# A causal attention and a squared-ReLU MLP on one core: another table of rank shifts for the scheduler

## The chip, the core and the metric

The kernel runs on one core of a Trainium2 chip. The metric is the device time of one execution in microseconds. Three runs of the kernel before gave 607.66, 607.70 and 609.86 us, a median of 607.7. The profiled execution is one more.

## The reference

`q`, `k` and `v` are float32 of shape (4, 12, 448, 64): four batches, twelve heads, 448 positions, 64 numbers a head. The MLP takes 1792 tokens of 768 numbers, with `w_in` (768 x 2048) and `w_out` (2048 x 768), which are float64 in the kernel's memory.

```python
scores = scale * np.matmul(q, k.transpose(0, 1, 3, 2))
mask = np.triu(np.ones((seq, seq), dtype=bool), k=1)
scores = np.where(mask, -1000000000.0, scores)
attn = np.exp(scores - np.max(scores, axis=-1, keepdims=True))
attn = attn / (np.sum(attn, axis=-1, keepdims=True) + 1e-09)
x = np.matmul(attn, v)          # heads side by side: (1792, 768)
h = np.maximum(x @ w_in, 0.0)
out = h * h @ w_out
```

## The kernel before

**Work.** Two heads (of 64) are handled together and called a head here, numbered 0 to 23; heads 0 to 11 belong to batches 0 and 1, 12 to 23 to batches 2 and 3. For a head, Q and K are loaded and turned over (on VectorE, `transposed`, or for some heads on TensorE, `turned_rows`); TensorE makes the scores in seven chunks of 64 queries (`softmax`, two steps of chunks for heads 0 to 11, one for the others); for each chunk VectorE adds the mask and takes the row maximum and ScalarE takes the exponential and its row sum (`exponential`); VectorE takes the reciprocals of the sums (`inverse`), GpSimd multiplies by them (`normalise`), TensorE turns P over (`transposed_p`), ScalarE or VectorE copies it out of PSUM, and TensorE multiplies by V (`times_v`).

The MLP runs on numbers that are split into a high and a low part (`split`), so that each product is three matmuls: high x high, high x low, low x high. The weights come in pieces (`piece`: a load, two conversions on ScalarE, three steps on VectorE, the split). For batches 0 and 1 the MLP is done directly, in four groups of 512 hidden columns (`h_unit`, lines 679 to 681, and `o_unit`, lines 1098 to 1100). For batches 2 and 3 a scheme of seven products in place of eight is used (`h_pair`, lines 860 to 864; `o_parts`, `o_seven` and `o_last`, lines 986 to 988), whose weight sums are made by GpSimd's accumulating loads (`added_up`) and split again; for the output weights the low half of the split is GpSimd's alone. In time: heads 0 to 11 with the first products between them until about 105 us, then heads 12 to 23 between the rest of the direct MLP until about 370 us, then the scheme of seven.

**What sets the order.** No instruction is written in its place. Each step is told to a planner with `plan.op`: its rank, the engines that could do it (`ways`) with a cost, what it reads and writes, and which buffers it takes and frees. `Plan.emit` then picks one step after the other: among all steps whose inputs are planned to be there, the one that could start first, and among those that could start at the same time the one with the lowest rank. It chooses the engine that would end it first. Two-operand instructions of VectorE and of GpSimd are marked as sharing a port and planned one after the other. The picked steps, in order of planned start, become the instruction streams of the engines and the DMA queues; each engine then works its stream in order and waits by semaphore for what a step reads. The planner's costs only set the order; nothing holds an instruction back on the chip but its inputs and its place in the stream.

**The table.** A step's rank is worked out from its place in the kernel. Afterwards `AMENDS` adds to it: an entry (first, end, more) adds `more` to the steps first to end - 1, numbered in the order in which `plan.op` was called.

```python
    def amend(self, table):
        for first, end, more in table:
            for o in self.ops[first:end]:
                o.rank += more
...
                key = (w[1], o.rank)
                if best is None or key < best[0]:
                    best = (key, o, w)
```

Which steps the numbers are, counted from the code: 0 to 49 head 0 (13 and 14 its turned K and Q, 15 and 22 its two score steps, 31 its reciprocals, 32 to 38 its normalisations, 39 to 46 its turned P, 47 times V); 50 to 94 head 1 (60 and 67 its score steps, 61 to 66 and 68 to 75 its exponentials, 76 its reciprocals); 95 to 139 head 2; 140 to 189 head 3; up to 547 heads 4 to 11; from 549 the first weight piece; up to 1,698 the direct MLP; from there heads 12 to 23, from 2,287 the parts of x, and the scheme of seven in the order in which it runs, up to 3,429.

Of the kernel before, what the change touches and what calls it, by code (L numbers as in the profile page):

```python
# [190 lines left out]
def kernel(  # L191
# [1017 lines left out]
    for gr, u in stages:  # L1209
# [5 lines left out]
            W = w_parts(gr, u, rank - LEAD, rank + 7 * CB * H_US - LEAD)  # L1215
            rank = h_pair(gr, u, W, rank, H_US, last)
    AMENDS = (
# [15 lines left out]
    )  # L1233
    plan.amend(AMENDS)
    with tc.manual_schedule():
# [32 lines left out]
```

## Time and profile before

| what | value |
|---|---|
| median of three runs | 607.7 us |
| the profiled execution's own time | 607.55 us |
| its span, first to last instruction | 605.4 us |
| busy: TensorE matmul, VectorE, ScalarE, GpSimd | 97%, 71%, 60%, 59% |
| granted TensorE clock, mean | 0.996 |
| data moved by DMA | 120.01 MB |

The span is what the trace covers; the execution's own time has some 2 us more around it. Engines are PE (TensorE's matmuls), PEld (its weight loads, beside PE), DVE (VectorE), ACT (ScalarE), POOL (GpSimd) and SP (SyncE, which issues most DMAs). L679 is line 679 of the kernel. A busy time of TensorE is modelled at its ends, since matmuls overlap in the array: the distance of two starts is the pace, the duration is longer.

### The profile page before, as it was taken

What the parts mean: (1) busy time and instruction counts of PE and PEld (TensorE: products, weight loads), DVE (VectorE), ACT (ScalarE), POOL (GpSimd) and SP (SyncE); (2) the same over time, 40 slices, a digit from 0 to 9 for tenths busy, and PEclk for the clock granted to TensorE, in tenths of its full rate; (3) what the DMA queues carried; (4) which work ended last, traced back from release to release, by engine and by line L of the source; (5) the groups of instructions that cost most, each with busy time, mean ns of one, the idle gap of its engine ahead of it and who ended that gap; (6) DMA issues with size and microseconds to landing.
All of it is one profiled execution on the core that took longest, in us unless ns stands there. A gap on an engine that the chain in (4) does not pass through costs nothing.

```text
span 605.4 us, 11455 instructions
## 1 busy us (share of the span) xinstructions
PE 586.6 (97%) x3766; PEld 514.5 (85%) x3766; DVE 427.2 (71%) x948; ACT 360.9 (60%) x887; POOL 356.4 (59%) x465
## 2 busy tenths in 40 slices
PE   3899999999999999999999999999999999999996
PEld 2577877898988998888898889999799999999995
DVE  4888796466876687666676518698896798778453
ACT  3899997674688555667547742268656645642400
POOL 2475772865577755967567844157675667776000
PEclk9999999999999999999999999999999999999999
DMA  9899444979799979977998668979757946762564
GB/s 157 185 230 190 101 113 102 256 237 308 189 282 297 266 193 227 285 208 229 251 264 266 233 204 241 273 241 211 188 120 169 229 104 138 177 162 55 168 100 84
DMA packets 190651, 120.01 MB, mean 198 GB/s; under 512 B 126016, under 2 KB 178560, under 8 KB 190592
## 3 DMA queue, kind: packets, MB, share of 16 engines
q1 hardware_dynamic: 169488, 107.99, 64.3%
q0 software_dynamic: 6912, 9.44, 10.2%
q10 hardware_dynamic: 14192, 1.85, 1.9%
q8 instruction: 30, 0.49, 0.3%
q14 instruction: 29, 0.24, 0.1%
HBM read 80.71 MB, written 38.54 MB: 197 GB/s over the span
## 4 chain that ended last, share of the span: by engine, by line
PE 91%; DVE 4%; DMA 1%; ACT 1%; SPq 0%; issue 0%; ACTq 0%; DVEq 0%
PE ps L482 7%; PE ps L679 7%; PE ps L1098 7%; PE ps L462 7%; PE ps L680 6%; PE ps L681 6%; PE ps L1100 6%; PE ps L1099 6%; PE ps L422 6%; PE ps L986 6%; PE ps L988 5%; PE ps L987 5%; PE ps L864 5%; PE ps L862 5%; PE ps L860 5%; DVE r L321 1%
## 5 line engine op out<-in xcount | busy, mean ns | idle before, releaser
L318 ACT ACTIVATE words<-words 128x384 f32<-128x384 f32 (+3 forms) x134 | 76.7, 599 | 25.4 <-DVE words L321 13.1
L448 POOL TENSOR_SCALAR ap<-ap,asm 128x64 f32<-128x64 f32 (+6 forms) x122 | 76.7, 647 | 24.6 <-DVE asm L516 17.9
L435 DVE CUSTOM_DVE_ANT_0 ps<-ps,mask 128x320 f32<-128x320 f32 (+6 forms) x168 | 68.4, 446 | 24.9 <-PE ps L422 20.6
L1098 PE MATMUL ps<-wo,g 128*128 128x384 f32 x224 | 77.0, 344 | 0.0
L1100 PE MATMUL ps<-wo,g 128*128 128x384 f32 x224 | 75.2, 336 | 0.0
L1099 PE MATMUL ps<-wo,g 128*128 128x384 f32 x224 | 75.2, 336 | 0.0
L679 PE MATMUL ps<-x,wi 128*128 128x448 f32 x192 | 74.2, 386 | 0.0
L680 PE MATMUL ps<-x,wi 128*128 128x448 f32 x192 | 70.3, 366 | 0.0
L681 PE MATMUL ps<-x,wi 128*128 128x448 f32 x192 | 70.3, 366 | 0.0
L439 ACT ACTIVATE ap<-ps,mx 128x64 f32<-128x64 f32 (+6 forms) x126 | 58.5, 479 | 14.2 <-DVE mx L435 13.4
L325 POOL TENSOR_TENSOR wi<-words,wi 128x384 fp32r<-128x384 f32 (+1 forms) x51 | 62.8, 1260 | 6.7 <-ACT wi L318 4.3
L318 ACT ACTIVATE r<-ps 128x448 f32<-128x448 f32 x63 | 33.9, 543 | 45.7 <-PE ps L864 16.1
L986 PE MATMUL ps<-g,wi 128*128 128x448 f32 x156 | 57.3, 368 | 1.5 <-ACT sa L318 1.5
L987 PE MATMUL ps<-g,wi 128*128 128x448 f32 x156 | 57.0, 366 | 0.0
L988 PE MATMUL ps<-g,wi 128*128 128x448 f32 x156 | 57.0, 366 | 0.0
L864 PE MATMUL ps<-x,wi 128*128 128x448 f32 x153 | 56.1, 367 | 0.0
L862 PE MATMUL ps<-x,wi 128*128 128x448 f32 x153 | 56.1, 367 | 0.0
L860 PE MATMUL ps<-x,wi 128*128 128x448 f32 x153 | 56.1, 366 | 0.0
L640 DVE TENSOR_SCALAR words<-words 128x384 int32<-128x384 int32 (+1 forms) x56 | 29.0, 520 | 32.4 <-ACT words L318 30.5
L331 POOL TENSOR_SCALAR wi<-words 128x512 fp32r<-128x512 f32 (+1 forms) x31 | 20.3, 663 | 50.5 <-DVE words L643 31.6
L318 ACT ACTIVATE apt<-ps 128x512 f32<-128x512 f32 x68 | 38.1, 603 | 17.4 <-PE ps L462 17.0
L321 DVE CUSTOM_DVE_ANT_0 words<-words 128x768 uint16<-128x768 uint16 (+1 forms) x56 | 39.7, 709 | 6.9 <-ACT words L318 3.9
(146 smaller groups left out, 1481.4 us busy)
## 6 DMA issues: line engine op xcount, KB each, us to landing
words<-in_moe_w_in_dram SPq DMA_DIRECT2D x24, 512.0 KB, 5.3
words<-in_moe_w_out_dram SPq DMA_DIRECT2D x32, 384.0 KB, 4.1
wo_split<-wo SPq DMA_DIRECT2D x26, 384.0 KB, 5.0
wi<-wo_split SPq DMA_DIRECT2D x25, 384.0 KB, 4.0
wo_whole<-words SPq DMA_DIRECT2D x32, 192.0 KB, 4.0
wi_split<-wi SPq DMA_DIRECT2D x24, 256.0 KB, 3.8
v<-in_v_dram SPq DMA_DIRECT2D x24, 192.0 KB, 4.4
wi_whole<-words SPq DMA_DIRECT2D x18, 256.0 KB, 4.6
```

The costliest lines, as they stand in the source:

```text
L318: return (ACT, t_act(n, psum, more), lambda: nc.scalar.activation(dst(), src(), func, **kw))
L679: nc.tensor.matmul(o, w[:, 0], x[:, 0], start=c == 0, stop=False)
L680: nc.tensor.matmul(o, w[:, 0], x[:, 1], start=False, stop=False)
L681: nc.tensor.matmul(o, w[:, 1], x[:, 0], start=False, stop=c == NP - 1)
L860: nc.tensor.matmul(o, w.t[:, 0, c], x[:, 0], start=begin and c == 0, stop=False, skip_group_check=True)
L862: nc.tensor.matmul(o, w.t[:, 0, c], x[:, 1], start=False, stop=False, skip_group_check=True)
L986: nc.tensor.matmul(o, w.t[:, 0, d], g.t[:, 0], start=start, stop=False, skip_group_check=True)
L987: nc.tensor.matmul(o, w.t[:, 0, d], g.t[:, 1], start=False, stop=False, skip_group_check=True)
L988: nc.tensor.matmul(o, w.t[:, 1, d], g.t[:, 0], start=False, stop=stop, skip_group_check=True)
L1098: nc.tensor.matmul(res(), g[:, 0], w[:, 0], start=f == 0, stop=False)
L1099: nc.tensor.matmul(res(), g[:, 0], w[:, 1], start=False, stop=False)
L1100: nc.tensor.matmul(res(), g[:, 1], w[:, 0], start=False, stop=f == GF - 1)
```

## The change

The table is replaced; nothing else is. The old one has 77 entries, the new one 237 shorter ones, and many entries of the old one come back cut into parts with different values. Below are the lines that the prediction speaks of.

```diff
-        (0, 25, 5.5), (25, 62, 9.6), (62, 65, 1.1), (65, 71, -2.8), (71, 107, -3.8), (107, 111, -4.9),
-        (111, 132, -7.2), (229, 237, -5.7), (274, 282, 6.9), (355, 369, 14.8), (369, 375, 15.9),
...
-        (460, 472, 13.1), (472, 495, 7.3), (495, 509, 3.7), (509, 563, 1), (563, 592, 6), (592, 603, -4.4),
-        (603, 614, 8.4), (621, 637, 15.6), (637, 666, 5.4), (877, 901, 3.8), (901, 920, 14.3),
-        (920, 937, 7.2), (937, 943, 9.3), (966, 970, 4.8), (970, 1080, 0.6), (1080, 1088, 1.1),
...
-        (2187, 2237, -0.4), (2237, 2263, -14.2), (2450, 2466, -5.6), (2466, 3233, -6.9), (3233, 3410, 3.5),
+        (0, 25, 5.5), (25, 31, 9.6), (31, 44, 13.9), (44, 61, 9.6), (61, 62, -25.2), (62, 65, -33.7),
+        (65, 71, -37.6), (71, 72, -38.6), (72, 107, -8), (107, 111, -9.1), (111, 113, -11.4),
+        (113, 119, -0.3), (119, 121, 3.9), (121, 125, -7.2), (125, 132, -14.4), (132, 134, -7.2),
+        (134, 147, 6.1), (147, 148, 5.7), (148, 150, 22.8), (155, 156, 6.9), (156, 164, 1.8),
...
+        (485, 495, 14), (495, 509, 10.4), (509, 557, 7.7), (557, 563, 1), (563, 570, 6), (570, 576, -11.2),
...
+        (637, 645, 14.9), (645, 666, 35.4), (666, 676, 30), (676, 716, 2.1), (720, 722, 5.5),
...
+        (877, 886, -1.8), (886, 892, -13.6), (892, 901, -5), (901, 904, 5.5), (904, 911, -0.4),
+        (911, 918, -11.1), (918, 919, -1.9), (919, 920, -9.1), (920, 921, -9.6), (921, 934, -13.1),
...
+        (2450, 2455, -8.1), (2455, 2458, -6.3), (2458, 2466, 4), (2466, 2469, 2.7), (2469, 2534, -6.6),
+        (2534, 2555, -2.1), (2555, 2571, -24.3), (2571, 2578, -6.9), (2578, 2581, -11), (2581, 2585, -0.7),
+        (2585, 2590, -3.2), (2590, 2610, -19.1), (2610, 2613, -12.1), (2613, 2632, -19.1),
...
+        (2959, 3233, -12.1), (3233, 3410, -1.7), (3410, 3412, -5.2),
```

## Rows read from the trace of the kernel before

**Rows 1.** The page's first part: busy us, share of the span, instructions.

```profile
PE 586.6 (97%) x3766; PEld 514.5 (85%) x3766; DVE 427.2 (71%) x948; ACT 360.9 (60%) x887; POOL 356.4 (59%) x465
```

**Rows 2.** Windows: length, busy us and instructions of each engine, clock, DMA share, GB/s.

```profile
30.00:45.00 15.00, 15.00 (x162) 11.53 (x160) 13.10 (x45) 14.54 (x44) 11.85 (x22) 1.00 1.01 231
...
405.00:420.00 15.00, 15.00 (x76) 13.80 (x75) 12.68 (x21) 11.29 (x23) 11.22 (x15) 1.00 0.95 233
420.00:435.00 15.00, 13.56 (x66) 11.91 (x64) 15.00 (x17) 9.79 (x19) 12.15 (x14) 1.00 0.86 201
...
465.00:480.00 15.00, 15.00 (x76) 13.84 (x75) 13.25 (x17) 9.83 (x20) 10.89 (x14) 1.00 0.92 201
...
600.00:606.00 6.00, 0.00 (x0) 0.00 (x0) 1.20 (x4) 0.22 (x1) 0.00 (x0) 0.79 0.37 77
```

**Rows 3.** Waits of TensorE: waiter <- what ended it: us, times, longest.

```profile
PE ps L422 <- DVE aqt L403: 6.8, 1, 6.8
PE ps L422 <- DVE asm L515: 3.4, 1, 3.4
PE ps L986 <- ACT sa L318: 1.5, 1, 1.5
```

**Rows 4.** Timeline of TensorE, first 45 us: start, us, instruction, count, idle before.

```profile
13.23 3.26 PE L422 MATMUL ps<-bkt,bqt 64*64 64x320 f32 x28 [3.38 <-DVE asm L515]
...
28.61 1.95 PE L482 MATMUL ps<-bpt,v 128*64 128x448 f32 x16
...
33.90 1.47 PE L462 MATMUL ps<-ident,ap 128*128 128x128 f32 x12
35.30 1.75 PE L422 MATMUL ps<-akt,aqt 64*64 64x448 f32 x28
36.98 1.95 PE L482 MATMUL ps<-apt,v 128*64 128x448 f32 x16
38.86 0.60 PE L389 MATMUL ps<-ident,rows 112*128 112x112 f32 x4
```

**Rows 5.** Timeline of VectorE at the start.

```profile
17.64 0.64 DVE L403 STREAM_TRANSPOSE aqt<-aq 128x448 f32<-128x448 f32 x1
18.21 0.60 DVE L435 CUSTOM_DVE_ANT_0 ps<-ps,mask 128x448 f32<-128x448 f32 x1
```

**Rows 6.** Timeline of ScalarE at the start.

```profile
19.19 0.60 ACT L318 ACTIVATE apt<-ps 128x512 f32<-128x512 f32 x1
19.66 0.65 ACT L439 ACTIVATE bp<-ps,mx 128x448 f32<-128x448 f32 x1
```

**Rows 7.** Matmuls by line: count, busy us, mean ns of one, idle before.

```profile
L679 PE MATMUL ps<-x,wi 128*128 128x448 f32 x192 | 74.2, 386 | 0.0
L681 PE MATMUL ps<-x,wi 128*128 128x448 f32 x192 | 70.3, 366 | 0.0
L1098 PE MATMUL ps<-wo,g 128*128 128x384 f32 x224 | 77.0, 344 | 0.0
L1100 PE MATMUL ps<-wo,g 128*128 128x384 f32 x224 | 75.2, 336 | 0.0
```

**Rows 8.** Timeline of VectorE, 408 to 440 us.

```profile
425.67 0.61 DVE L321 TENSOR_TENSOR g<-f,g 128x448 fp32r<-128x448 f32 x1
426.21 4.12 DVE L321 TENSOR_TENSOR r<-r,f 128x448 f32<-128x448 f32 x1
...
432.39 3.06 DVE L321 TENSOR_TENSOR r<-r,r 128x448 f32<-128x448 f32 x1
```

**Rows 9.** Timeline of GpSimd there: the first and the last of three.

```profile
426.57 1.34 POOL L325 TENSOR_TENSOR wi<-words,wi 128x384 fp32r<-128x384 f32 x1
...
428.50 1.33 POOL L325 TENSOR_TENSOR wi<-words,wi 128x384 fp32r<-128x384 f32 x1
```

**Rows 10.** Timeline of ScalarE there.

```profile
434.46 0.52 ACT L318 ACTIVATE sa<-ps 128x448 f32<-128x448 f32 x1
```

45 rows, old and new, of the table AMENDS are left out of this document.

## The prediction

> **What bounds the kernel now.** I read the page's first two parts, then a table of 15 us windows, then the waits of TensorE, then the timelines of the two places where TensorE waits. TensorE works 586.6 of the 605.4 us of the span [rows 1]. The window table says where the rest is: all 26 windows from 30 to 420 us show it busy 15.00 of 15.00, the first and the last of them stand in the group, and so do the nine from 450 to 585; 420 to 435 lacks 1.44, and the last 5.4 us of the span have no matmul at all [rows 2]. Its waits are few: 6.8 us until the first transposed Q is there, 3.4 us before head 1's scores, 1.5 us late in the kernel behind a copy of ScalarE [rows 3]. So the profiled execution is 2.15 us outside the span (607.55 less 605.4), 6.8 before the first matmul, about 593.2 of TensorE from there to 600.0, and 5.4 of tail. The number of matmuls does not depend on the table: only what keeps them apart can move. (607.55 stands 0.15 below the median of 607.7; the sum below is against 607.55.)
>
> Three things keep them apart. **The start.** From head 1's scores at 13.23 to head 1's product with V at 28.61 are 15.38 us. TensorE does 68 score matmuls there (two heads and 12 of a third), 32 transposes, one product with V and 8 transposes of rows. Later the same work starts at a settled pace: 28 scores in 36.98 - 35.30 = 1.68, a product with V in 38.86 - 36.98 = 1.88, 12 transposes in 35.30 - 33.90 = 1.40, and 4 row transposes last 0.60 [rows 4]. That makes 68 x 0.060 + 32 x 0.117 + 1.88 + 1.2 = 10.9, so 4.5 us are waiting inside the start, beside the 3.4 ahead of it. **Breaks.** The first matmul of a triple that can follow a break lasts longer: L679 386 ns against L681's 366, x192, is 3.8 us; L1098 344 against L1100's 336, x224, is 1.8 us [rows 7]. Together 5.6 us hang on how often the order switches TensorE between attention and products. **The late wait.** At 426.21 VectorE's subtraction takes 4.12 us and at 432.39 its addition 3.06, where its neighbour of the same shape takes 0.61 [rows 8]; beside the first of them three two-operand instructions of GpSimd lie end to end, 426.57 to 429.83 [rows 9]. ScalarE's queue stands behind VectorE's results, so its copy of a finished PSUM bank to `sa` starts only at 434.46 [rows 10], and TensorE waits 1.46 of its 1.5 us of [rows 3] for that bank.
>
> **The change part by part.** I number the steps in the order in which the program calls `plan.op` and subtract the old table from the new one, step by step. 1,919 of 3,430 steps get another rank, by 7.8 on average up or down. No operation is added or removed; the rank decides only between steps that the planner could start at the same time, so a shift changes an order, or nothing, or (where two engines may take the step) the engine.
>
> (a) Start, steps 0 to 189 (heads 0 to 3). Head 1's exponentials and its second score step (61 to 71) go forward by 34.8, to ranks between -25 and -13, ahead of everything there. Head 0's reciprocal, its seven normalisations and most of its P transposes (31 to 43) go back by 4.3. Head 2's exponentials 113 to 120 go back by 6.9 to 11.1, head 2's Q and K transposes forward by 4.2, and the first weight piece (549 to 556) back by 6.7. Today VectorE does head 2's Q transpose (17.64) before the last and widest row maximum of head 1 (18.21) [rows 5], and ScalarE copies a transposed P of head 0 (19.19) before head 1's last exponential (19.66) [rows 6]. With the new ranks both swap: the exponential goes from 19.66 to 19.19, 0.47 earlier, and with it head 1's reciprocal, the GpSimd normalisations behind it and the transposes that wait for them. One more row maximum of head 2 (0.30 us) now stands behind head 3's Q transpose instead of ahead of it. 0.47 + 0.30 gives -0.8, which I take. The ends: at best all 4.5 us of waiting go; at worst a step that went back (head 0's normalisations, head 2's exponentials, the weight piece) makes TensorE wait once more, and the nearest row to such a wait is the 3.4 us ahead of head 1's scores [rows 3]. So -4.5 to +3.4. I stay near the rows that swap. The cover for the weight piece is attention itself: TensorE comes to the first triple of products only after head 1's product with V.
>
> (b) The steps of 30 to 405 us: group 0's second half later by 30 (645 to 675), group 1's first products earlier by 9 to 25 (886 to 933), the second batches' heads 12 to 23 shifted one by one. TensorE is never idle there [rows 2] because products fill what attention leaves; the cover is the stock of ready products, and the window just before the end of the first twelve heads is as full as the rest. A step moved there earns nothing unless it changes the number of breaks. I take 0, between -1.4 (a quarter of the 5.6 us of breaks gone, my estimate) and +1.4 (a quarter more). DMA issues on SyncE's queue move too (heads 3, 6, 7, 15, 18 to 20); what waits behind them is the same filler-covered attention, so 0 as well, with the same ends.
>
> (c) The late wait. The GpSimd instructions at 426.57 to 429.83 are the low halves of weight sums of the first output turn; with the rest of that chain, its accumulating loads included (2590 to 2631), they go forward by 12.2 (three of them by 5.2), from ranks 435 to 438 to 423 to 426. VectorE's subtraction that they hold up has rank 430 before and after. So where the planner put GpSimd behind VectorE's chain it now puts it ahead, and the activations of the next pair (2555 to 2570), which stand before the `sa` copies on ScalarE's queue, go forward by 17.4 while the additions they wait for (2534 to 2554) go back by 4.8. The planner sees a GpSimd instruction and a two-operand VectorE one as sharing a port, and with the new ranks it plans the wait instead of meeting it. I take the 1.46 us of TensorE's wait as gone: -1.5. Ends: -1.5, and +3.5 if another such run of three lands in the chain (4.12 less 0.6 [rows 8]). VectorE is busy without a gap from 420 to 435 (15.00 of 15.00 [rows 2]), so there is no cover for a further one.
>
> The Trainium skill, "SBUF — State Buffer", section "SBUF: two separate sides", says that VectorE with two SBUF inputs and GpSimd share one port pair by an exclusive lock held for a whole instruction, and that the loser waits until it ends. Read as one instruction at a time, that would make the 4.12 us about 1.6 (0.6 and one of the three at their spacing of 0.97), and a further collision would cost about 1.0 instead of 3.5; the trace agrees that one blocks the other but not on the length, since one VectorE instruction waited out three [rows 8, 9].
>
> (d) After step 2,959 (from 475 us): one shift of -5.2 for all up to 3,411. A common shift swaps nothing, TensorE is full there, and the last 18 steps, which make the tail of 5.4 us, are not in either table: 0.
>
> Sum: -0.8 + 0 - 1.5 + 0 = -2.3; 607.55 - 2.3 = 605.2.
>
> **Rivals.** A, more of the waiting goes: half of the start's 4.5 (2.2), the late 1.5 and a quarter of the breaks (1.4) make -5.1: 602.4. For it: the entries lie thick exactly where these rows are. Against: the 3.4 us ahead of head 1's scores cannot move, since head 0's exponentials and head 1's transposes on VectorE keep their ranks.
> B, the order moves and the time does not: ScalarE waits for something else at 434, and the start is paced by the work of VectorE and ScalarE whatever its order: 607.5. For it: 26 full windows. Against: the two swaps of (a) need no luck.
> C, slower: the run of GpSimd instructions, moved ahead, falls into VectorE's gapless chain at 412 to 432 once more. Today's two blocked instructions cost VectorE 3.5 + 2.5 = 6.0 us and TensorE 1.46, so the cushion between them is some 4.5 us; it is used up, and each further run of three costs 3.5: 611.0 with one, 614.5 with two. It decides from the point where VectorE loses more than 6.0 us to blocked instructions before 435. For it: the shift sends these instructions into a stretch where every VectorE instruction is of the two-operand kind. Against: the planner serialises the two.
>
> **How the numbers follow.** Forecast 605.2, chance 0.38, its own range 603.9 to 606.6. A 0.27, B 0.18, C 0.17. A measurement here can tell about 0.5% from no change: 604.7 and 610.7 against 607.7. A is faster, B the same, C slower; of the forecast's own range about a third lies under 604.7. Faster 0.27 + 0.12 = 0.39, same 0.26 + 0.18 = 0.44, slower 0.17. From 601.5 to 610.5 leaves out C and a small part of A, 2 in 10.
>
> **What would show it.** (a): head 1's last exponential ahead of the P copy on ScalarE, and the product with V of head 1 before 28.0. (b): the means of L679 and L1098 within 5 ns of now, all windows from 30 to 405 at 15.00. (c): no wait of TensorE behind ScalarE's `sa` copy; if VectorE instructions of over 1.5 us before 435 sum to more than today, C. (d): last stretch and tail as before, 5.4 us without a matmul. The prediction is wrong if TensorE idles in a window that is full now, or if the breaks change by more than a quarter.

## The result, and the profile after

| | before | changed |
|---|---|---|
| median in the comparison | 609.10 us (607.66 to 611.50) | 603.58 us (603.15 to 606.17) |
| ratio, 95% interval | | 0.9914 [0.9885, 0.9943] |
| the profiled execution's own time | 607.55 us | 606.17 us |
| its span | 605.4 us | 604.3 us |

The changed kernel is 0.57 to 1.15% faster. The profiled execution shows less of it than the medians do: of before it is shorter than all six timed runs, of the changed kernel it is the longest of six. So the changed kernel was run and profiled once more (604.73 us, span 603.0), and below both traces of it are read.

Busy time of the changed kernel, as in [rows 1]: TensorE's is the same, VectorE and GpSimd have each 8 us less.

```profile
PE 587.0 (97%) x3766; PEld 513.8 (85%) x3766; DVE 418.8 (69%) x951; ACT 361.8 (60%) x889; POOL 348.1 (58%) x460
```

Its windows, as in [rows 2]. From 420 to 435 TensorE is now full and VectorE no longer is (13.09 of 15.00), but four windows that were full no longer are: 30 to 45 lacks 0.59, 45 to 60 lacks 0.44, and 405 to 420 and 465 to 480 some 0.3 each. (In the second trace 30 to 45 lacks 0.27 and 405 to 420 lacks 0.38.)

```profile
30.00:45.00 15.00, 14.41 (x138) 10.86 (x139) 13.59 (x44) 13.48 (x43) 10.98 (x20) 1.00 0.97 205
45.00:60.00 15.00, 14.56 (x146) 10.84 (x144) 11.86 (x39) 14.70 (x46) 7.62 (x13) 1.00 1.01 181
...
405.00:420.00 15.00, 14.70 (x72) 13.16 (x72) 12.24 (x21) 11.44 (x24) 9.20 (x11) 1.00 0.90 223
420.00:435.00 15.00, 15.00 (x75) 13.60 (x74) 13.09 (x20) 11.46 (x24) 9.63 (x13) 1.00 0.89 210
...
465.00:480.00 15.00, 14.74 (x73) 13.32 (x72) 8.64 (x15) 7.46 (x16) 7.80 (x10) 1.00 0.71 176
```

TensorE's waits, as in [rows 3]. The wait behind ScalarE's copy to `sa` is gone. New are a wait of 0.6 at L679 for a copy of ScalarE (at 32 us), two waits for a load of split weights, and one for `sb` just before the end.

```profile
PE ps L1063 <- DVE sb L321: 0.5, 1, 0.5
...
PE ps L860 <- DMA wi<-wi_split: 0.3, 1, 0.3
...
PE ps L986 <- DMA wi<-wo_split: 0.3, 1, 0.3
```

At the start ScalarE does what was forecast: head 1's last exponential (18.94) stands ahead of the copy of head 0's P (19.84); in [rows 6] it was the other way round. (The last one is another chunk now: step 75, 128 wide, in place of step 62, 448 wide.) TensorE's product with V of head 1 starts at 27.03, not 28.61 [rows 4].

```profile
18.94 0.37 ACT L439 ACTIVATE bp<-ps,mx 128x128 f32<-128x128 f32 x1
...
19.84 1.10 ACT L318 ACTIVATE apt<-ps 128x512 f32<-128x512 f32 x2
```

```profile
27.03 1.95 PE L482 MATMUL ps<-bpt,v 128*64 128x448 f32 x16
```

The breaks, as in [rows 7], are what they were: 386 and 343 ns.

```profile
L1098 PE MATMUL ps<-wo,g 128*128 128x384 f32 x224 | 76.8, 343 | 0.0
...
L679 PE MATMUL ps<-x,wi 128*128 128x448 f32 x192 | 74.1, 386 | 0.6 <-ACT aqt L318 0.6
```

VectorE's late sums, 400 to 605 us (count, busy us, mean ns of one). First before, then the changed kernel: 12 of them took 1,349 ns on average, now 11 take 679, where one that nothing holds up takes some 610. The longest from 408 to 440 us was 4.12 [rows 8] and is 2.33.

```profile
L321 DVE TENSOR_TENSOR r<-r,r 128x448 f32<-128x448 f32 x12 | 16.2, 1349 | 0.1
```

```profile
L321 DVE TENSOR_TENSOR r<-r,r 128x448 f32<-128x448 f32 x11 | 7.5, 679 | 0.1
```

```profile
422.02 2.33 DVE L321 TENSOR_TENSOR f<-f,r 128x448 f32<-128x448 f32 x1
```

The tail, on VectorE, before and then the changed kernel (its second trace). Before, a sum and a turn of another output block (599.56 and 600.22) stand between the last product's sum and the two copies that end the chain. In the changed kernel they are not there any more.

```profile
598.34 0.69 DVE L321 TENSOR_TENSOR sb<-ps,sb 128x256 f32<-128x256 f32 x2 [1.74 <-PE ps L988]
599.56 0.62 DVE L321 TENSOR_TENSOR sb<-ps,sb 128x448 f32<-128x448 f32 x1 [0.53 <-PE ps L988]
600.22 0.65 DVE L1036 STREAM_TRANSPOSE words<-sb 128x448 f32<-128x448 f32 x1
600.79 0.44 DVE L1072 COPY words<-ps 128x128 f32<-128x128 f32 x2
```

```profile
597.95 0.69 DVE L321 TENSOR_TENSOR sb<-ps,sb 128x256 f32<-128x256 f32 x2 [1.13 <-PE ps L988]
599.16 0.48 DVE L1072 COPY words<-ps 128x128 f32<-128x128 f32 x2 [0.53 <-PE ps L1063]
```

**Where the time goes, of ten kernels alike.** For each step on TensorE I took its start in the timeline, less the sum of the settled durations of all steps ahead of it (0.61 us for a triple of first-product matmuls, 1.88 for a product with V, and so on; 574.35 in all). What is left, the lag, grows only where TensorE loses time. The table has the first matmul, what the lag grew by in four stretches (the first one without the first matmul), and the time behind the last matmul; a row adds up to the span less 574.8 (574.35 and some 0.4 for the last step itself).

| kernel | first matmul | to 60 us | 60 to 405 | 405 to 495 | 495 to the end | tail |
|---|---|---|---|---|---|---|
| before | 6.75 | 11.37 | 4.90 | 2.26 | -0.05 | 5.46 |
| before, again | 6.92 | 11.15 | 4.91 | 2.24 | -0.04 | 5.46 |
| changed | 6.73 | 11.39 | 5.07 | 1.66 | 0.88 | 3.81 |
| changed, again | 7.20 | 10.35 | 5.08 | 0.86 | 0.86 | 3.83 |
| tail_swap | 7.18 | 11.35 | 4.91 | 3.18 | 0.68 | 3.83 |
| spread | 7.37 | 10.83 | 5.36 | 1.71 | -0.05 | 5.46 |
| graft_late | 6.99 | 11.37 | 4.88 | 1.25 | 0.87 | 3.82 |
| two_edits | 7.27 | 11.39 | 4.91 | 1.63 | 0.69 | 3.83 |
| early_turn | 7.03 | 10.95 | 5.09 | 1.09 | 0.87 | 3.82 |
| start_only | 7.14 | 12.42 | 6.94 | 1.71 | 6.66 | 5.65 |

The kernels of the table that are not named so far are those of the experiments. Two more, middle_only and late_only, read in the same way, lose 6.9 and 8.3 us from 405 to 495.

### The profile page after: what moved, and what is told of

The parts are those of the page before. It is cut to its first block, busy times and chain, and to the rows that moved or that the text cites. A ratio compares the mean times of both kernels' runs of the same rounds, so it can differ in the third digit from the quotient of the medians.

```text
span 604.3 us, 11456 instructions
## 1 busy us (share of the span) xinstructions
PE 587.0 (97%) x3766; PEld 513.8 (85%) x3766; DVE 418.8 (69%) x951; ACT 361.8 (60%) x889; POOL 348.1 (58%) x460
## 4 chain that ended last, share of the span: by engine, by line
PE 90%; DMA 4%; ACT 2%; SPq 2%; issue 1%; DVE 0%; ACTq 0%; DVEq 0%
PE ps L1098 7%; PE ps L679 7%; PE ps L1100 6%; PE ps L1099 6%; PE ps L681 6%; PE ps L680 6%; PE ps L482 6%; PE ps L462 6%; PE ps L986 6%; PE ps L988 6%; PE ps L987 6%; PE ps L422 5%; PE ps L860 5%; PE ps L864 5%; PE ps L862 5%; DMA words<-in_moe_w_in_dram 2%
## 5 line engine op out<-in xcount | busy, mean ns | idle before, releaser
L318 ACT ACTIVATE words<-words 128x384 f32<-128x384 f32 (+3 forms) x140 | 79.8, 597 | 27.9 <-DVE words L321 15.3
L448 POOL TENSOR_SCALAR ap<-ap,asm 128x64 f32<-128x64 f32 (+6 forms) x123 | 74.6, 626 | 30.6 <-DVE asm L516 27.7
L435 DVE CUSTOM_DVE_ANT_0 ps<-ps,mask 128x448 f32<-128x448 f32 (+6 forms) x168 | 68.4, 446 | 19.2 <-PE ps L422 12.9
L679 PE MATMUL ps<-x,wi 128*128 128x448 f32 x192 | 74.1, 386 | 0.6 <-ACT aqt L318 0.6
L439 ACT ACTIVATE ap<-ps,mx 128x448 f32<-128x448 f32 (+6 forms) x126 | 59.2, 487 | 15.0 <-DVE mx L435 11.1
L325 POOL TENSOR_TENSOR wi<-words,wi 128x384 fp32r<-128x384 f32 (+1 forms) x44 | 52.6, 1204 | 11.8 <-ACT wi L318 6.6
L986 PE MATMUL ps<-g,wi 128*128 128x448 f32 x153 | 56.0, 366 | 0.3 <-DMA wi<-wo_split 0.3
L987 PE MATMUL ps<-g,wi 128*128 128x448 f32 x153 | 56.0, 366 | 0.0
L988 PE MATMUL ps<-g,wi 128*128 128x448 f32 x153 | 56.0, 366 | 0.0
L331 POOL TENSOR_SCALAR wi<-words 128x384 fp32r<-128x384 f32 (+1 forms) x39 | 26.9, 689 | 46.6 <-DVE words L643 23.0
L321 DVE CUSTOM_DVE_ANT_0 words<-words 128x768 uint16<-128x768 uint16 (+1 forms) x56 | 42.3, 755 | 5.8 <-ACT words L318 3.3
L318 ACT ACTIVATE apt<-ps 128x512 f32<-128x512 f32 x65 | 35.6, 611 | 14.5 <-PE ps L462 14.4
```

The source lines that it names most:

```text
L318: return (ACT, t_act(n, psum, more), lambda: nc.scalar.activation(dst(), src(), func, **kw))
L679: nc.tensor.matmul(o, w[:, 0], x[:, 0], start=c == 0, stop=False)
L986: nc.tensor.matmul(o, w.t[:, 0, d], g.t[:, 0], start=start, stop=False, skip_group_check=True)
L987: nc.tensor.matmul(o, w.t[:, 0, d], g.t[:, 1], start=False, stop=False, skip_group_check=True)
L988: nc.tensor.matmul(o, w.t[:, 1, d], g.t[:, 0], start=False, stop=stop, skip_group_check=True)
```

## The experiments

Each kernel was timed in five rounds beside runs of the kernel before, and profiled.

**1. Both kernels unchanged, once more** (again, before_again). No edit.

> The changed kernel once more, nothing edited. Its first trace (execution 606.2 us) shows 5.4 -> 3.8 us of tail, the late wait gone and about 1 us of new waits between 30 and 60 us; the other timed runs were 603.2 to 604.3. Theory 'stalls vary': a second trace with 603 to 604 us has the same tail and no late wait, and lacks the waits of 30 to 60 us. Theory 'clock or pace': the second trace has the same waits and all its matmuls a little closer. Ratio to before 0.988 to 0.995 in either case.

Measured: 604.95 us (604.59 to 605.70), ratio 0.9936 [0.9911, 0.9961]. The second trace has the same tail and no late wait, and of 0.9 us of waits from 30 to 60 us 0.3 is left, as 'stalls vary' had it.

> The kernel before once more, nothing edited, for a second trace of it: its timed runs lie between 607.1 and 612.4 us, those of the changed kernel between 603.2 and 606.2. Theory 'same stalls': the second trace has the late wait of 1.5 us and the tail of 5.4 us again, and TensorE's lag at the end is within 1 us of the first. Theory 'the old order is fragile': the second trace has waits that the first lacks, of 1 to 4 us, after 405 us.

Measured: 608.58 us (607.50 to 611.56), 0.9998 [0.9980, 1.0016]. Its trace has the tail again and a late wait of 1.7: 'same stalls'. So the gain is 0.6 to 0.9%. The two traces of the changed kernel have the same instructions in the same order, and yet differ by 1.0 us up to 60 and by 0.8 from 405 to 495: a difference of 1 us or less in one stretch of one trace says little by itself. The runs of before spread over 4.8 us (606.93 to 611.73 in one set of 27), those of the changed kernel over 1.1 here and 3.0 in the first comparison.

**2. One part of the new table at a time** (start_only, middle_only, late_only). The parts are laid over the old table; for the first of them:

```diff
-    plan.amend(AMENDS)
+    PARTS = ((NEW, 0, 549), (OLD, 549, 3430))
+    plan.amend([(max(a, lo), min(b, hi), m) for table, lo, hi in PARTS for a, b, m in table])
```

For the other two the new table stands for the steps 549 to 2,286, and for those from 2,287 on.

> New table for steps 0 to 548 (heads 0 to 11), old table for the rest. Prediction's theory: 0.5 to 1 us faster than before, from 15 to 30 us, the late wait of 1.5 us still there, tail 5.4. Rival theory from the two traces (the lag of TensorE at 60 us was the same 18.1 us in both): no change, within 0.5 us.

Measured: 617.25 us (614.96 to 619.57), 1.0139 [1.0106, 1.0173].

> New table for steps 549 to 2286 (weight pieces, direct MLP, heads 12 to 23), old for the rest. Prediction's theory: 0, within 1.4 us. Rival theory: the gain of the whole change that the traces do not place (some 3 us) sits here, as fewer waits between 30 and 405 us.

Measured: 613.64 us (613.10 to 614.13), 1.0076 [1.0051, 1.0102].

> New table for steps from 2287 on (parts of x and the scheme of seven), old for heads and direct MLP. Prediction's theory: the late wait goes, 1.5 us faster, tail unchanged at 5.4. Theory from the two traces: the late wait goes (2 us of TensorE's lag between 420 and 450) and the tail shortens by 1.1 to 1.6 us because the last product on TensorE is again the one that ends the kernel: 3 us faster in all. Rival theory 'only the whole table': the late order depends on when the earlier plan ends, and the late wait stays.

Measured: 612.86 us (607.73 to 615.31), 1.0049 [1.0021, 1.0076].

Each third of a change that gains 0.6 to 0.9% loses 0.5 to 1.4% alone; every reading on record had said faster or no change. Each trace shows the same sight late in the kernel: a VectorE instruction held for over 4 us beside instructions of GpSimd, and a wait of TensorE behind it. In start_only, whose entries are for steps that run up to some 105 us, the largest loss is TensorE's wait of 3.6 us for a VectorE sum at 503, and VectorE is late: its instruction at 497.91 took 5.18 beside a run of GpSimd's. Waits of TensorE, VectorE and GpSimd there:

```profile
PE ps L986 <- DVE sa L321: 3.6, 1, 3.6
```

```profile
497.91 5.18 DVE L321 TENSOR_TENSOR g<-r,g 128x448 fp32r<-128x448 f32 x1
```

```profile
497.90 2.29 POOL L325 TENSOR_TENSOR wi<-words,wi 128x384 fp32r<-128x384 f32 x2
499.88 0.79 POOL L331 TENSOR_SCALAR wi<-words 128x384 fp32r<-128x384 f32 x1
500.36 1.28 POOL L325 TENSOR_TENSOR w<-words,w 128x384 fp32r<-128x384 f32 x1
501.33 1.28 POOL L325 TENSOR_TENSOR wi<-words,wi 128x384 fp32r<-128x384 f32 x1
```

In middle_only it is a VectorE instruction of 4.19 us at 445.70 and a wait of 3.2 behind it; in late_only one of 4.39 at 423.95 (beside two sums and a DMA issue of GpSimd's, 424.33 to 427.84), a wait of 2.4, and one of 2.1 for a load of split weights:

```profile
445.70 4.19 DVE L321 TENSOR_TENSOR g<-r,g 128x448 fp32r<-128x448 f32 x1
```

```profile
423.95 4.39 DVE L321 TENSOR_TENSOR g<-r,g 128x448 fp32r<-128x448 f32 x1
```

```profile
PE ps L860 <- DVE r L321: 2.4, 1, 2.4
PE ps L986 <- DMA w<-wo_split: 2.1, 1, 2.1
```

An entry for the start moves late steps too: each step's planned start depends on all before it, so of the 146 late steps on GpSimd 49 go to another engine in start_only and 50 others come, and of the 97 that stay 29 stand in another place. The parts can't be added: the same entries give another order in another plan. What late_only loses goes with the clock: of its 12 runs the two with a mean granted clock of 1.000 took 607.73 and 608.27 us, within before's range, and the ten at 0.997 or less took 609.55 to 615.31.

**3. The tail alone** (tail_swap). One entry is added to the old table; the instruction streams are before's up to the last products:

```diff
         (2187, 2237, -0.4), (2237, 2263, -14.2), (2450, 2466, -5.6), (2466, 3233, -6.9), (3233, 3410, 3.5),
+        (3406, 3412, -5.2),
```

> Old table, and steps 3406 to 3411 (the last product but one of the output, its addition and its turn) 5.2 earlier in rank, the same place against the last 18 steps that the new table gives them. Nothing before 595 us changes. Prediction's part (d), 'a common shift swaps nothing in the tail': no change, span 605.4 or as before. Theory 'the tail got its order from this': tail without matmul 3.8 instead of 5.4 us, TensorE's last matmul 0.5 later, span 1.1 us shorter: 0.2% of the time, at the edge of what five rounds tell, but plain in the trace.

Measured: 607.65 us (606.37 to 609.39), 0.9969 [0.9952, 0.9985]. The tail falls by 1.63, from 5.46 to 3.83, and costs the wait of 0.5 for `sb` that the changed kernel has too; in the table the stretch from 495 to the end is 0.73 longer for it, so 0.9 is left. The late wait, whose order was not touched, is longer in this trace than in [rows 3]: the same instructions in the same order gave 1.5 us, 1.7 in before_again, and 2.7 here.

```profile
PE ps L986 <- ACT sa L318: 2.7, 1, 2.7
```

**4. The run of three broken** (spread). Before's order is written out as a list of (step, engine) and followed as it stands, with two of the three GpSimd instructions of [rows 9] moved back: step 2613 behind step 2498, step 2590 behind step 2700. (Lines of kernels with a written list are 10 lower than in before.)

```diff
-    plan.amend(AMENDS)
...
-        plan.emit()
+        plan.emit(LISTED, ((2613, 2498), (2590, 2700)))
```

> The order of the kernel before, instruction for instruction on every engine and queue, except that GpSimd's second and third subtraction of the run at 426.57 to 429.83 us (steps 2613 and 2590) come later in its stream, behind steps 2498 and 2700, so that the run is one instruction. Theory 'a run of GpSimd subtractions blocks VectorE for its whole length, and that is the late wait': the subtraction of 4.12 us takes 1.3 to 1.9, what follows on VectorE and ScalarE is 2 to 2.5 us earlier, and TensorE's wait of 1.5 us is gone: 1.5 to 2 us faster. Rival 'the wait is ScalarE's order, not the block': the subtraction is short, the wait stays. Rival 'the block only moves': the next VectorE instruction of two operands takes the 2 to 3 us and the wait stays.

Measured: 606.61 us (605.49 to 607.56), 0.9955 [0.9938, 0.9972]. The subtraction that took 4.12 in [rows 8] takes 2.18, beside the one GpSimd sum that is left. But step 2590, moved back, now stands end to end with two sums that followed (433.80), and beside this new run of three VectorE is held for 3.25 us at 434.25: the rival 'the block only moves' has part of it. First VectorE, then GpSimd, then the wait of TensorE, 0.8 in place of 1.5 (the theory had it gone):

```profile
428.27 2.18 DVE L311 TENSOR_TENSOR r<-r,f 128x448 f32<-128x448 f32 x1
434.25 3.25 DVE L311 TENSOR_TENSOR g<-r,g 128x448 fp32r<-128x448 f32 x1 [0.54 <-ACT g L308]
```

```profile
428.62 1.34 POOL L315 TENSOR_TENSOR wi<-words,wi 128x384 fp32r<-128x384 f32 x1
...
433.80 3.21 POOL L315 TENSOR_TENSOR wi<-words,wi 128x384 fp32r<-128x384 f32 x3
```

```profile
PE ps L976 <- ACT sa L308: 0.8, 1, 0.8
```

The span did not shrink (605.4): this trace gained 0.55 from 405 to 495 and had lost as much ahead of it, where no order was touched (first matmul 0.62 later, 0.54 less up to 60, 0.46 more from 60 to 405). The runs did, by 0.3 to 0.6%.

**5. The late order transplanted** (graft_late). A written list again: the steps below 2,287 in before's order and on its engines, those from 2,287 in the changed kernel's, merged by planned start; nothing is planned anew.

```diff
-    plan.amend(AMENDS)
+    LISTED = (
...
-        plan.emit()
+        plan.emit(LISTED)
```

> A written order of steps in place of the planner's choice: steps 0 to 2286 in the order and on the engines that the kernel before has them, steps from 2287 on in the order and on the engines of the changed kernel. Nothing is planned anew. Theory 'a table is worth only the order it gives, and the late order is where the gain is': no late wait, tail 3.8, at most one VectorE instruction of over 2 us after 405, 2.5 to 4 us faster than before, the time of the changed kernel within 1 us, although the new entries for these steps alone made the kernel 0.5% slower. Theory 'the late order fits only the early order it was found with': waits of 2 to 5 us after 405 us, no gain or slower.

Measured: 605.59 us (604.97 to 606.08), 0.9935 [0.9913, 0.9957], level with the changed kernel run again (0.9936); tail, late wait and holds are as its theory had them. The start is before's, and its wait of 1.1 at L422 <- bpt, in before's trace too, is there; the late wait behind `sa` is not.

```profile
PE ps L412 <- ACT bpt L308: 1.1, 1, 1.1
...
PE ps L850 <- DMA wi<-wi_split: 0.4, 1, 0.4
```

So the gain lies, as far as these runs can tell, in the order from step 2,287 on, and it can be carried over as an order where it could not be as a part of the table.

**6. The two local edits together** (two_edits). The list is that of tail_swap, with the two moves of spread.

```diff
-        plan.emit()
+        plan.emit(LISTED, ((2613, 2498), (2590, 2700)))
```

> The kernel before with two local edits and nothing else of the change: the output turn of the last-but-one product (steps 3406 to 3409) ahead of the last product, as in the kernel with the one entry for the tail, and two GpSimd instructions of the late run of three moved behind other work, as in the kernel with that run broken. All other instructions stay on the engine and in the place that the kernel before gives them. Theory (the gain is these two local places, and the other 1,900 shifts are there without effect): the two gains add up, 0.9969 x 0.9955 = 0.9924 of the kernel before, 604.5 to 605.5 us, level with the changed kernel at 0.9936. Late wait of TensorE at most 1 us, tail 3.8 us, span 604.2 or less. Rival (the changed kernel's gain is in the late order as a whole, the many VectorE instructions that GpSimd no longer holds up): the two edits reach half of it, 0.9955 or 606.7 us, and the waits of TensorE from 405 to 500 us still sum to 1.5 us or more.

Measured: 605.48 us (604.67 to 606.27), 0.9941 [0.9919, 0.9963]. The interval holds the theory's 0.9924 and the rival's 0.9955, so the runs don't decide between them. The trace doesn't decide either: the late wait is 1.0 and the tail 3.83, as the theory had them, but the span is 604.5 and not 604.2 or less; the rival's waits of 1.5 us or more from 405 to 500 are not there (1.0 in all), and 405 to 495 loses 1.63 us, where the changed kernel loses 1.66 and 0.86.

```profile
PE ps L976 <- ACT sa L308: 1.0, 1, 1.0
```

What is sure: two edits of a few steps can't be told from the whole new table (0.9936).

**7. A step further at the start** (early_turn). The changed kernel's order as a list, with seven moves: head 1's last two loads of K ahead of the first two loads of V (the moves of its Q loads, 56 and 57, leave their queue in the same order), its K turned (58) behind head 0's Q (14) and its Q (59) behind head 0's first row maximum (16), head 2's K (103) behind head 1's last one (74).

```diff
-        plan.emit()
+        plan.emit(LISTED, ((52, 51), (53, 52), (56, 55), (57, 56), (58, 14), (59, 16), (103, 74)))
```

> The changed kernel's order with a local edit at the start, to see what the first waits of TensorE are worth that the table could not move: head 1's last two loads of K are issued ahead of the first two loads of V, VectorE turns head 1's K over before head 0's row maxima and its Q after the first of them (both stand behind all seven now), and head 2's K behind head 1's row maxima. Nothing else moves. VectorE has 1.9 us without work at 7.2 us and 1.0 us at 14.5 us, ScalarE 2.7 us at 13.4 us, and TensorE 3.2 us behind head 0's scores. Theory (TensorE's lag at the start is the order of VectorE's first 30 us, so work put into VectorE's gaps comes back on TensorE): head 1's scores start by 11.5 us in place of 13.7, the lag at 60 us falls by 1.0 to 2.0 us, and the time to 0.9905 of the kernel before, 603.5 us or less. Rival (the start is bound by the loads: Q and K of head 1 are not there before 9.5 us, and the loads of V behind them make TensorE wait later): lag and time within 0.5 us of the changed kernel, with a wait for a load in place of the one for VectorE.

Measured: 604.68 us (604.11 to 605.40), 0.9931 [0.9911, 0.9951], no better than the changed kernel. The theory fell, and the rival had the outcome but not the reason. The loads were there (VectorE turns head 1's K over at 8.07, first fence), and head 1's scores started at 10.19 in place of 13.68; but the lag at 60 us is 10.95, within what the changed kernel's two traces show. Then TensorE in the changed kernel, and in early_turn:

```profile
8.07 0.65 DVE L393 STREAM_TRANSPOSE bkt<-bk 128x448 f32<-128x448 f32 x1 [1.02 <-DMA bk<-in_k_dram]
```

```profile
13.68 3.26 PE L422 MATMUL ps<-bkt,bqt 64*64 64x320 f32 x28 [3.22 <-DVE asm L515]
16.88 2.56 PE L462 MATMUL ps<-ident,ap 128*128 128x128 f32 x16
19.47 1.75 PE L422 MATMUL ps<-akt,aqt 64*64 64x320 f32 x28
```

```profile
10.19 1.75 PE L412 MATMUL ps<-bkt,bqt 64*64 64x320 f32 x28
14.77 1.53 PE L452 MATMUL ps<-ident,ap 128*128 128x128 f32 x4 [2.84 <-POOL ap L438]
...
19.98 3.27 PE L412 MATMUL ps<-akt,aqt 64*64 64x320 f32 x28
```

The wait of 3.2 us came back as one of 2.84, for GpSimd's normalisation of head 0. Head 1's scores took 1.75 in place of 3.26, but head 2's took 3.27 in place of 1.75, and the 16 transposes between them, 2.56 in the changed kernel, lie from 14.77 to 19.98. Windows of early_turn and then of the changed kernel (the number before the DMA share is the granted clock): the clock fell to 0.50, that is 1.2 GHz, after the wait, where the changed kernel kept 1.00, 2.4 GHz.

```profile
19.00:23.00 4.00, 4.00 (x33) 2.57 (x32) 2.02 (x7) 2.69 (x6) 3.45 (x7) 0.50 0.60 113
```

```profile
19.00:23.00 4.00, 3.48 (x40) 1.98 (x40) 3.65 (x12) 3.89 (x12) 2.37 (x6) 1.00 0.60 111
```

No kernel here beats the changed one; early_turn is level with it.

## Why the prediction was right, and where it was not

The forecast was 605.2, for the sum -2.3; the medians were 603.58, which lies 0.3 under the forecast's own range, and 604.95. Of the changed kernel's two traces the second is 2.5 us shorter than before's span, the first 1.1. That 2.5 is so near the forecast is in part luck: it is made of -1.0 at the start, -1.4 from 405 to 495, -1.6 and +0.9 at the end, which the forecast had at nothing, and +0.6 of a later first matmul and the middle.

**(a) Start, -0.8: the swaps happened, the gain shows once.** Head 1's last exponential stands ahead, in the first trace 0.72 earlier than the last one in [rows 6], and its product with V starts before 28.0 us, as the prediction asked. Up to 60 us this is worth 1.0 in the second trace and nothing in the first, which lost 0.9 from 45 to 50 us (TensorE busy 4.57 of 5.00 there, full in the second). graft_late, which has none of it, is level with the changed kernel, so at most a few tenths of a per cent hang on it. The best end, 4.5 us of waiting inside the start, was misread: TensorE's waits there sum to 1.7 (0.35, 0.28 and 1.1 at 22.1, 24.5 and 27.7), and the rest is matmuls at a slower pace. Head 1's 28 scores took 3.26 [rows 4] where the settled 28 take 1.68, at a granted clock of 0.50 in before:

```profile
13.00:15.00 2.00, 1.77 (x20) 1.48 (x24) 1.05 (x4) 0.00 (x0) 1.32 (x4) 0.50 0.99 271
```

In the changed kernel they took 3.10 and 3.26 although the clock of that window reads 1.00; why they are slow stays open. Early_turn took the wait ahead of them away, and TensorE waited for head 0's normalisation instead, at the lower clock behind it. That head 0's chain of exponentials and normalisations bounds the start in any order is argued, not shown. Rival A's half of the start's waiting was not to be had by these moves.

**(b) Middle, 0: right in the sum, not in its sign.** From 60 to 405 it is 4.90 before, 5.07 and 5.08 after, and the means of the breaks [rows 7] are within 1 ns. But the prediction also named TensorE idle in a full window as a sign of being wrong, and from 30 to 60 us that came: 0.59 and 0.44 in the first trace, 0.27 in the second. So products did not fill everything that attention leaves there: a first-product matmul itself waited 0.6 us, behind a copy of ScalarE (L679 <- `aqt`). In start_only 60 to 405 lost 2.0 us more.

**(c) Late wait, -1.5: the mechanism holds, the size was smaller in one trace.** The wait for `sa` is gone, and VectorE has no hold of over 2.4 us from 408 to 440. Two of the three sums (2593 and 2590) were indeed put ahead, to 418.11, where VectorE waits for TensorE until 418.88 and then reads PSUM; the third (2613) went the other way, behind 431, and stands apart:

```profile
418.11 2.00 POOL L325 TENSOR_TENSOR wi<-words,wi 128x384 fp32r<-128x384 f32 x2 [0.31 <-ACT wi L318]
```

From 405 to 495 the gain is 0.6 and 1.4, since a load of split weights is late in its place (0.3 and 0.4 at 405 to 420). Spread shows the cause by itself, for about half of the wait: with the run of three broken, the hold goes from 4.12 to 2.18 and the wait to 0.8 (1.0 in two_edits), where the three traces with the run have 1.5, 1.7 and 2.7. What makes the rest was not tried. So an instruction is held back by more than its inputs and its place in the stream. On this the prediction weighed the Trainium skill, "SBUF — State Buffer", section "SBUF: two separate sides", which says that the lock on the shared ports is held for one whole instruction. Where one GpSimd sum stands beside the VectorE instruction the trace agrees (2.18, where 0.61 of its own and 1.34 of the other make 1.95); where several lie end to end it does not: VectorE waited out three of them in [rows 8, 9], and 5.18 us at 497.91 in start_only. The further collision that rival C priced at 3.5 us was not in the changed kernel, but each of its thirds has one of that size.

**(d) Tail, 0: wrong.** The step that failed is "A common shift swaps nothing". The shift of -5.2 is common to the steps 2,959 to 3,411, but not to the 18 behind them, and against those it does swap: steps 3,406 to 3,409 are in the old table's last entry; its 3.5 gives them ranks of 617.1 to 618.9, among the last product's 616.0 to 617.8, and -1.7 puts them ahead, at 611.9 to 613.7. That moved a VectorE sum, a turn and the four stores behind them from after the last product's sums to ahead of them, which is 1.6 off the tail, less 0.7 to 0.9 that TensorE loses from 495 to the end, the new wait among it. tail_swap shows it with one entry.

**What the trace could not show.** The sum was made against a profiled execution of 607.55 us. In the comparisons before's medians were 608.4 to 609.8, and the changed kernel's lay 5.5 and 4.3 us below them: about twice the forecast's 2.3, and more than the traces' 1.1 and 2.5. So part of the gain is in executions of before that were not profiled. Their granted clock is on record: of 67 timed runs of before, 30 took 609.5 us or more, and 28 of these had a mean clock of 0.996 or less; of the 37 shorter ones three had. That fits a clock that falls behind a wait in some executions only, as the last section shows it in late_only, but where it falls in before is not shown: both its traces are of 607.5 us. (A low mean alone does not make a run long: spread has 0.994 to 0.999 at 605.5 to 607.6 us.) That the late wait varies from execution to execution is seen (1.5, 1.7 and 2.7 for the same order), and the kernels without that run of three spread less (2.1 us in 10 runs of spread, 1.1 in 6 of graft_late; before 4.8 in 27, tail_swap, which keeps the run, 3.0 in 12). That these holds make before's longer runs is argued, not shown.

## What to carry to other kernels

A shift that is common to many steps still swaps them against the steps that don't get it: look at the borders of an entry, above all the last one, where nothing comes behind to hide the order. Where a planner works from costs, an entry may be worth something only in the plan that it was found in, as with the three parts here; to keep what was found, carry over the order itself, not a part of the table. And before a wait is moved forward, ask what TensorE meets next: early_turn took away one wait of 3.2 us and got another of 2.8, at the lower clock behind it.

## What the runs showed of the hardware that was not expected

After some waits TensorE's matmuls come at half the pace, and after others of about the same length they don't. In late_only, after the wait of 2.43 us that ends at 429.45, the first triple is at the old pace, then the matmuls are 0.37 apart and not 0.20:

```profile
429.45 0.47 PE L860 MATMUL ps<-x,wi 128*128 128x448 f32 x1 [2.43 <-DVE r L321]
...
430.50 0.57 PE L862 MATMUL ps<-x,wi 128*128 128x448 f32 x1
430.87 0.57 PE L864 MATMUL ps<-x,wi 128*128 128x448 f32 x1
```

The granted clock there is 0.55 as the mean of two microseconds (0.50 would be 1.2 GHz throughout); in tail_swap, behind a wait of 2.67 us, it is 1.00, as after before's 1.46. Late_only's stretch first, then that of tail_swap:

```profile
430.00:432.00 2.00, 2.00 (x8) 1.77 (x7) 1.69 (x3) 1.28 (x3) 0.40 (x1) 0.55 1.07 251
```

```profile
436.00:438.00 2.00, 1.62 (x8) 1.52 (x9) 1.85 (x3) 1.48 (x4) 0.29 (x1) 1.00 0.55 128
```

So a wait can cost more than its length: in start_only the lag grew by 5.1 us from 495 to 510, of which the wait was 3.6, and in late_only by 8.3 from 405 to 495, of which its two waits were 4.6. What decides whether the clock falls was not tried.
